# Bonus sums of the first two chunks by TensorE, state decay on ScalarE, one weight split less ahead of the first tile

## The chip, the cores and the metric

One core of a Trainium2 chip runs the whole kernel. The metric is the device time of one execution in microseconds. Engines are named as the profile names them: PE is TensorE, DVE VectorE, ACT ScalarE, POOL GpSimd, SP SyncE, which here only issues transfers.

## The reference, cut to what matters

```
for t in range(S):                       # attention with decay, B 2, H 8, S 768, D 48
    cur = u[None] * kt outer vt          # the bonus: only for the step itself
    y[t] = rt . (state + cur)
    state = w * state + kt outer vt
x = y as [1536 tokens, 384]
x = sum over 4 experts e: p[:, e] * (relu(x @ w1[e]) @ w2[e])     # hidden 1024
out = elu(x @ w_in) @ w_out              # hidden 2048, alpha 1
```

All in 32-bit floats. The share of the bonus in y at token t and head h is a0[t, h] * v[t], with a0[t, h] the sum over the head's 48 elements of r * u * k.

## The kernel before, in words

The attention runs in 12 chunks of 128 tokens, six for each batch. In each chunk r is scaled by the powers of w (table `T`) and k by their inverses (table `Kd`) in the layout with tokens along the columns (`rkT`, lines 204 to 207). `s2` multiplies them to scores, and `s2p` copies the scores under a mask (`copy_predicated`) into the tile `A`, whose diagonal holds a0. `s1u` makes `uk` = r * u * k in the layout with tokens along the partitions (`rk`, 384 columns of r and 384 of k), `s1d` reduces it to a0, and the diagonals are written as the identity times a0: the even heads on GpSimd (line 242), the odd ones on ScalarE (`s1e`, line 248) in chunks 2 and 3, all on GpSimd after that. For chunks 0 and 1, `A` is zeroed at the start, and the bonus comes in at the end instead: `va` = v * a0 on VectorE, added by TensorE in `s3i`. `s3s` brings the state to the next chunk: `Z` = sum of the chunk + old state, `S` = `Z` times w to the 128th, both on VectorE.

Ahead of the loop all of chunks 0 and 1 is done, and part of chunk 2. Then `layers` runs six hidden layers (four experts, two halves of the last one) over token tiles; the first tile has 256 tokens and eight steps f = 0 to 7. At step f: `st1` (line 684), `evac` (`hh` on ScalarE, `hl` on VectorE), then a piece of the attention from the list `steps` (f = 0: scores of chunk 2, preparation of chunk 3; f = 1: `s3(2)`; f = 2: scores of chunk 3; f = 3: `s3(3)`; f = 4: preparation of chunk 4; f = 6: scores of chunk 4; f = 7: `s4(3)`, which writes `xh` and `xl` of tokens 256 to 511 from the tile `xs`), then `st2` of step f - 2 (line 722), and last `work(0.9)`, which makes one split.

A split takes one weight slice `raw` (128 x 768), writes its high part `wh` on ScalarE and its low part `wl` on VectorE (or on the engine `weng`), and then issues the load of the slice three further on, since there are three `raw` buffers. The slices are numbered here from 0 in the order in which they are made: (0,1,0), (0,1,1), (0,2,0), (0,1,2), (0,2,1), (0,1,3), (0,2,2), (0,2,3). The middle number is 1 for `st1` and 2 for `st2`, and the last is f // 2. Eight slots hold eight split slices, and the first tile uses all eight.

Each engine takes its instructions in the order written. SP's queue holds the loads in program order; `s3` of an odd chunk stores `yT` to `xd`, and the load of `xs` behind it waits for that store to land.

## Time and profile before

| what | value |
|---|---|
| median of 3 runs | 653.62 us (653.33 to 654.23) |
| the profiled execution | 653.03 us, of which the span 651.1 us |
| TensorE matmuls | 639.2 us, 98% of the span |
| VectorE, ScalarE, GpSimd | 334.1, 216.7, 214.6 us |

The profile gives, for one execution, start and duration of each instruction, the idle time ahead of it with the instruction that ended it, and for a transfer the time from issue to landing. Times in timelines count from the start of the span. PEld is the loading of weights into TensorE.

### The profile page before, as it was taken

To read this page: it belongs to the slowest core of one execution; us is meant where nothing else is said; L and a number is where in the kernel's file an instruction comes from. 1 tells how busy PE (TensorE), PEld (TensorE's weight loads), DVE (VectorE), ACT (ScalarE), POOL (GpSimd) and SP (SyncE) were. 2 spreads that over 40 slices of the span, in tenths; PEclk is the share of its full clock that TensorE was granted. 3 is DMA by queue.
4 is the path that set the end of the run, shared out by engine and by line. 5 is a ranking of instruction groups with operands and counts; after the bars stand their busy time and mean duration, and the time that the engine had idled before them with its cause. 6 is when DMAs were issued, how large, how long until landed. Compare 5 with 4: busy or idle time off the path is not lost.

```text
span 651.1 us, 9435 instructions
## 1 busy us (share of the span) xinstructions
PE 639.2 (98%) x3825; PEld 537.1 (82%) x3825; DVE 334.1 (51%) x472; ACT 216.7 (33%) x370; POOL 214.6 (33%) x178
## 2 busy tenths in 40 slices
PE   9799999999999999999999999999999999999996
PEld 6699998988888888888888888888888888888885
DVE  7975665346454545554545456566667553222221
ACT  5532222333211132211122112123645564544441
POOL 7954773100031212130311122242754434333331
PEclk9999999999999999999999999999999999999998
DMA  8883562343230233421216231318441342001011
GB/s 257 248 288 120 160 175 76 144 122 122 72 97 1 98 120 118 159 88 48 98 49 229 92 138 52 97 35 312 188 146 44 102 145 98 0 1 49 1 49 53
DMA packets 27735, 73.10 MB, mean 112 GB/s; under 512 B 3154, under 2 KB 8580, under 8 KB 27684
## 3 DMA queue, kind: packets, MB, share of 16 engines
q1 hardware_dynamic: 22928, 59.80, 28.6%
q10 hardware_dynamic: 4756, 12.61, 5.1%
q8 instruction: 32, 0.52, 0.3%
q14 instruction: 19, 0.16, 0.1%
HBM read 55.47 MB, written 16.93 MB: 111 GB/s over the span
## 4 chain that ended last, share of the span: by engine, by line
PE 95%; DVE 3%; issue 1%; ACT 0%; DVEq 0%
PE ph L684 45%; PE po L722 45%; PE pa L263 1%; PE ph L102 1%; PE pa L334 1%; PE pa L325 1%; DVE rkT L206 1%; PE po L334 1%; PE ph L285 1%; DVE A L270 0%; DVE wl L533 0%; DVE a L232 0%; DVE acc L772 0%; DVE hl L697 0%; DVE xl L496 0%
## 5 line engine op out<-in xcount | busy, mean ns | idle before, releaser
L722 PE MATMUL po<-hh,wh 128*128 128x512 f32 (+1 forms) x480 | 177.4, 370 | 0.0
L722 PE MATMUL po<-hl,wh 128*128 128x512 f32 (+1 forms) x480 | 176.5, 368 | 0.0
L722 PE MATMUL po<-hh,wl 128*128 128x512 f32 (+1 forms) x480 | 176.5, 368 | 0.0
L684 PE MATMUL ph<-xh,wh 128*128 128x512 f32 (+1 forms) x480 | 174.5, 369 | 1.5 <-DVE xl L496 0.8
L684 PE MATMUL ph<-xh,wl 128*128 128x512 f32 (+1 forms) x480 | 173.8, 368 | 0.0
L696 ACT ACTIVATE hh<-ph 128x512 fp32r<-128x512 f32 (+1 forms) x112 | 60.2, 537 | 269.3 <-PE ph L684 266.4
L697 DVE SCALAR_TENSOR_TENSOR hl<-ph,hh 128x512 fp32r<-128x512 f32 (+1 forms) x112 | 68.5, 613 | 154.6 <-ACT hh L696 154.2
L684 PE MATMUL ph<-xl,wh 128*128 128x512 f32 (+1 forms) x480 | 124.6, 368 | 0.0
L684 PEld LDWEIGHTS ph<-xh,wh 128*128 128x128 f32 x480 | 90.4, 188 | 17.6 <-DVE hl L697 1.0
L722 PEld LDWEIGHTS po<-hh,wh 128*128 128x128 f32 x480 | 90.4, 188 | 16.5 <-issue 1.5
L722 PEld LDWEIGHTS po<-hl,wh 128*128 128x128 f32 x480 | 90.4, 188 | 15.0
L722 PEld LDWEIGHTS po<-hh,wl 128*128 128x128 f32 x480 | 90.4, 188 | 15.0
L684 PEld LDWEIGHTS ph<-xh,wl 128*128 128x128 f32 x480 | 90.5, 188 | 14.9
L709 POOL TENSOR_TENSOR hl<-g,hh 128x512 fp32r<-128x512 f32 x48 | 63.2, 1318 | 117.4 <-ACT hh L708 109.3
L684 PEld LDWEIGHTS ph<-xl,wh 128*128 128x128 f32 x480 | 85.9, 188 | 15.2 <-DVE xl L496 0.2
L595 POOL TENSOR_TENSOR nl<-a,wide 128x768 fp32r<-128x768 f32 x16 | 29.9, 1870 | 173.5 <-issue 105.8
L706 DVE SCALAR_TENSOR_TENSOR g<-m,ph 128x512 f32<-128x512 f32 x48 | 33.0, 686 | 104.4 <-ACT m L704 100.1
L744 POOL TENSOR_TENSOR acc<-acc,t 128x512 f32<-128x512 f32 x27 | 34.2, 1297 | 72.8 <-DVE t L743 72.8
L708 ACT CAST hh<-g 128x512 fp32r<-128x512 f32 x48 | 29.9, 622 | 43.0 <-DVE g L706 43.0
L703 ACT ACTIVATE m<-ph 128x512 f32<-128x512 f32 x48 | 28.7, 598 | 43.4 <-PE ph L684 36.4
L533 DVE TENSOR_TENSOR wl<-raw,wh 128x768 fp32r<-128x768 f32 x31 | 30.7, 1004 | 7.2 <-ACT wh L532 6.7
L704 ACT ACTIVATE m<-m 128x512 f32<-128x512 f32 x48 | 30.4, 632 | 1.5
(116 smaller groups left out, 478.9 us busy)
## 6 DMA issues: line engine op xcount, KB each, us to landing
raw<-in_ws_dram SPq DMA_DIRECT2D x32, 384.0 KB, 4.3
wide<-in_ws_dram SPq DMA_DIRECT2D x16, 768.0 KB, 5.1
w<-nh ACTq DMA_DIRECT2D x16, 384.0 KB, 2.5
w<-nl ACTq DMA_DIRECT2D x16, 384.0 KB, 5.6
wh<-w SPq DMA_DIRECT2D x16, 384.0 KB, 6.0
wl<-w SPq DMA_DIRECT2D x16, 384.0 KB, 6.8
rk<-in_rkv_dram SPq DMA_DIRECT2D x12, 384.0 KB, 6.4
rkT<-in_rkT_dram SPq DMA_DIRECT2D x10, 448.0 KB, 6.0
```

The costliest lines, as they stand in the source:

```text
L533: self.weng.tensor_tensor(out=lo, in0=t, in1=hi.bitcast(F32), op=ALU.subtract)
L595: nc.gpsimd.tensor_tensor(out=lo, in0=af, in1=cf, op=ALU.add)
L684: nc.tensor.matmul(ph[:, 0:n], a[:, kk, c0:c0 + P], b[:, kk], start=q == 0, stop=q == 3 * KD - 1)
L696: nc.scalar.activation(hh[:, 0:n], ph[:, 0:n], AF.Relu)
L697: nc.vector.scalar_tensor_tensor(out=hl[:, 0:n], in0=ph[:, 0:n], scalar=0.0, in1=hh[:, 0:n].bitcast(F32), op0=ALU.max, op1=ALU.subtract)
L703: nc.scalar.activation(m, ph, AF.Relu, scale=-1.0)
L704: nc.scalar.activation(m, m, AF.Exp, scale=-1.0)
L706: nc.vector.scalar_tensor_tensor(out=gg, in0=m, scalar=-1.0, in1=ph, op0=ALU.add, op1=ALU.max)
L708: nc.scalar.copy(hh, gg)
L709: nc.gpsimd.tensor_tensor(out=hl, in0=gg, in1=hh.bitcast(F32), op=ALU.subtract)
L722: nc.tensor.matmul(po, a[:, ff, i * P:(i + 1) * P], b[:, 0:n], start=f == 0 and q == 0 and not i * n % TB, stop=f == NF - 1 and q == 2 and ...
L744: nc.gpsimd.tensor_tensor(out=a, in0=a, in1=t[:, 0:n], op=ALU.add)
```

## The change

The bonus sums a0 of chunks 0 and 1 are made from the scaled `rkT`: VectorE multiplies r by k (`s1p`), and TensorE sums each head's 48 rows with a table `U2` = u * w as the moving operand (`s1a`); the factor w makes up for the powers that the scaling left. The result is written to the diagonals of `A` (even heads GpSimd, odd heads ScalarE), as in chunks 2 and 3. So r by token isn't loaded for these chunks (`load_kv`), `va` and `s3i` go, and `A` isn't zeroed. `vp` has two buffers. The table `Kt` comes from a reversed copy of `T` (`Tr`), not from `Kd`. The decay is multiplied in ahead, by ScalarE (`s3w`, four activations), so that VectorE has one addition for each chunk. Four warm matmuls are left out. The second split ahead of the loop, on GpSimd, is left out. The first `ph` buffer of the loop is the other one.

```diff
--- before.py
+++ after.py
@@ -74,11 +74,15 @@
         self.ub = c.tile([P, DM], F32, name="ub")
         self.ur = c.tile([1, DM], F32, name="ur")
         self.one = c.tile([1, P], F32, name="one")
-        self.vp = c.tile([P, 112 + 160 * H], F32, tag="xs", name="vp")
+        self.vp = [
+            c.tile([P, 112 + 160 * H], F32, tag="xs", name="vp0"),
+            g.xp.tile([P, 112 + 160 * H], F32, tag="acc2", name="vp1")]
         self.Sp = c.tile([P, 96 + 192 * NP], F32, tag="yT", name="Sp")
         self.mask = c.tile([P, P], U8, name="mask")
-        self.rkT, self.rk, self.v, self.va, self.pa, self.st, self.px = ({} for _ in range(7))
-        self.S = self.Sv = self.zero = None
+        self.ud = c.tile([P, NP], F32, name="ud")
+        self.U2 = c.tile([P, NP, 2], F32, name="U2")
+        self.rkT, self.rk, self.v, self.a0, self.pa, self.st, self.px = ({} for _ in range(7))
+        self.S = self.wS = self.zero = None
 
         self.own = [(self.ps, f"pa{i}") for i in range(3)] + [(g.pop, "po2")]
         self.banks = self.own[:3] + [(g.pop, f"po{i}") for i in range(KD)] + [(g.php, "ph0")]
@@ -116,6 +120,11 @@
         self.rk[ci] = t = self.p3.tile([P, 2, DM], F32, tag="rk", name="rk")
         self.g.nc.sync.dma_start(out=t, in_=self.g.rkv[ci, :, 0:2])
 
+    def load_kv(self, ci):
+        t = self.p3.tile([P, 2, DM], F32, tag="rk", name="rk")
+        self.g.nc.sync.dma_start(out=t, in_=self.g.rkv[ci, :, 1:3])
+        self.rk[ci], self.v[ci] = t, t[:, 1]
+
     def load_v(self, ci):
         self.v[ci] = t = self.p4.tile([P, DM], F32, tag="v", name="v")
         self.g.nc.sync.dma_start(out=t, in_=self.g.rkv[ci, :, 2])
@@ -123,15 +132,14 @@
     def setup_loads(self):
         g, nc = self.g, self.g.nc
         nc.scalar.dma_start(out=self.ur, in_=g.u.rearrange("h d -> (h d)").rearrange("(o n) -> o n", o=1))
+        nc.scalar.dma_start(out=self.ud, in_=g.ud)
         nc.sync.dma_start(out=self.wd, in_=g.wd)
         for ci in range(2):
             self.load_T(ci)
             self.load_T2(ci, 0)
             self.load_T2(ci, 1)
-        self.load_rk(0)
-        self.load_v(0)
-        self.load_rk(1)
-        self.load_v(1)
+        self.load_kv(0)
+        self.load_kv(1)
 
     def setup_tables(self):
         g, nc = self.g, self.g.nc
@@ -160,6 +168,12 @@
                 out=Kd[:, :, n:2 * n], in0=Kd[:, :, 0:n],
                 in1=Kd[:, :, n - 1:n].to_broadcast([P, NP, n]), op=ALU.mult)
 
+    def setup_u2(self):
+        for j in range(2):
+            a = slice(64 * j, 64 * j + D)
+            self.g.nc.gpsimd.tensor_tensor(
+                out=self.U2[a, :, j], in0=self.ud[a], in1=self.T[a, :, 1], op=ALU.mult)
+
     def setup_masks(self):
         nc = self.g.nc
 
@@ -172,17 +186,16 @@
 
     def setup_zeros(self):
         nc = self.g.nc
-        for t in self.A:
-            for j in range(2):
-                nc.scalar.copy(t[:, j].rearrange("s p t -> s (p t)"), self.zero)
-        for i in range(0, self.vp.shape[1], 512):
-            t = self.vp[:, i:min(i + 512, self.vp.shape[1])]
-            nc.scalar.copy(t, self.zero[:, 0:t.shape[1]])
+        for vp in self.vp:
+            for i in range(0, vp.shape[1], 512):
+                t = vp[:, i:min(i + 512, vp.shape[1])]
+                nc.scalar.copy(t, self.zero[:, 0:t.shape[1]])
 
     def setup_rest(self):
         nc = self.g.nc
         for t in self.kp:
             nc.gpsimd.memset(t.rearrange("t p j d -> t (p j) d")[:, :, D:64], 0.0)
+        nc.gpsimd.memset(self.U2, 0.0)
         nc.gpsimd.memset(self.Sp, 0.0)
         for t in self.Sb:
             nc.gpsimd.memset(t[:, :, D:64], 0.0)
@@ -195,8 +208,10 @@
     def setup_kt(self):
         g, nc = self.g, self.g.nc
         pk = self.bank()
+        Tr = self.c.tile([P, NP, P], F32, name="Tr")
+        nc.scalar.copy(Tr, self.T[:, :, P - 1::-1])
         for p in range(NP):
-            nc.tensor.transpose(pk[:, p * P:(p + 1) * P], self.Kd[:, p, :], g.ident)
+            nc.tensor.transpose(pk[:, p * P:(p + 1) * P], Tr[:, p, :], g.ident)
         nc.scalar.copy(self.Kt.rearrange("t p j d -> t (p j d)"), pk)
 
 
@@ -207,7 +222,7 @@
         self.st.setdefault(ci, {})["rk"[i]] = self.rkT[ci][:, i]
 
     def heads(self, ci, i):
-        return self.rk[ci][:, i].rearrange("t (h d) -> t h d", h=H)
+        return self.rk[ci][:, i if ci > 1 else 0].rearrange("t (h d) -> t h d", h=H)
 
 
     def s1k(self, ci):
@@ -227,26 +242,35 @@
 
 
     def s1d(self, ci):
-        nc = self.g.nc
-        a0 = self.p2.tile([P, H], F32, tag="a0", name="a0")
-        nc.vector.tensor_reduce(out=a0, in_=self.st[ci]["uk"], axis=AX.X, op=ALU.add)
-        if ci < 2:
-
-            self.va[ci] = va = self.p2.tile([P, DM], F32, tag="va", name="va")
-            nc.vector.tensor_tensor(
-                out=va.rearrange("t (h d) -> t h d", h=H), in0=self.v[ci].rearrange("t (h d) -> t h d", h=H),
-                in1=a0.rearrange("s (h o) -> s h o", o=1).to_broadcast([P, H, D]), op=ALU.mult)
-            return
-        self.a0 = a0
+        self.a0[ci] = a0 = self.p2.tile([P, H], F32, tag="a0", name="a0")
+        self.g.nc.vector.tensor_reduce(out=a0, in_=self.st[ci]["uk"], axis=AX.X, op=ALU.add)
         for j in range(1 if ci < 4 else 2):
-            nc.gpsimd.tensor_tensor(
-                out=self.A[ci % 2][:, j], in0=self.g.ident.rearrange("s (a t) -> s a t", a=1).to_broadcast([P, NP, P]),
-                in1=a0.rearrange("s (p j o) -> s p j o", j=2, o=1)[:, :, j].to_broadcast([P, NP, P]), op=ALU.mult)
+            self.s1g(ci, j)
+
+    def s1g(self, ci, j):
+        self.g.nc.gpsimd.tensor_tensor(
+            out=self.A[ci % 2][:, j], in0=self.g.ident.rearrange("s (a t) -> s a t", a=1).to_broadcast([P, NP, P]),
+            in1=self.a0[ci].rearrange("s (p j o) -> s p j o", j=2, o=1)[:, :, j].to_broadcast([P, NP, P]), op=ALU.mult)
 
     def s1e(self, ci):
         for p in range(NP):
             self.g.nc.scalar.activation(
-                self.A[ci % 2][:, 1, p, :], self.g.ident, AF.Copy, scale=self.a0[:, 2 * p + 1:2 * p + 2])
+                self.A[ci % 2][:, 1, p, :], self.g.ident, AF.Copy, scale=self.a0[ci][:, 2 * p + 1:2 * p + 2])
+
+
+    def s1p(self, ci):
+        self.pr = self.p2.tile([P, NP, P], F32, tag="pr", name="pr")[0:112]
+        st = self.st[ci]
+        self.g.nc.vector.tensor_tensor(out=self.pr, in0=st["r"][0:112], in1=st["k"][0:112], op=ALU.mult)
+
+    def s1a(self, ci):
+        nc = self.g.nc
+        pq = self.g.php.tile([P, 512], F32, tag="ph1", name="ph1")[:, 0:H]
+        for p in range(NP):
+            nc.tensor.matmul(
+                pq[:, 2 * p:2 * p + 2], self.pr[:, p, :], self.U2[0:112, p, :], start=True, stop=True)
+        self.a0[ci] = a0 = self.p2.tile([P, H], F32, tag="a0", name="a0")
+        nc.scalar.copy(a0, pq)
 
     def s1(self, ci):
         self.s1h(ci, 0)
@@ -291,24 +315,26 @@
         nc = self.g.nc
         if pu is None:
             return
-        old, v = self.Sv, nc.vector
-        w = self.T[0:112, :, P:P + 1]
         src = pu[0:112, 0:NP * D].rearrange("q (p e) -> q p e", p=NP)
         if not ci:
-            self.Sv = self.Sp[0:112, 96:].rearrange("q (p n) -> q p n", p=NP)[:, :, 0:96].rearrange(
+            Sv = self.Sp[0:112, 96:].rearrange("q (p n) -> q p n", p=NP)[:, :, 0:96].rearrange(
                 "q p (j e) -> q p j e", j=2)
             for j in range(2):
                 a = slice(64 * j, 64 * j + D)
-                v.tensor_tensor(out=self.Sv[a, :, j, :], in0=src[a], in1=w[a].to_broadcast([D, NP, D]), op=ALU.mult)
+                nc.scalar.copy(Sv[a, :, j, :], src[a])
             return
         self.S = self.Sb[ci % 2]
-        self.Sv = self.S[0:112, :, 0:D]
+        out = self.S[0:112, :, 0:D]
         if ci % NCB:
-            z = self.p2.tile([P, NP, D], F32, tag="Z", name="Z")[0:112]
-            for a, o in [(slice(0, 64), old[:, :, 0]), (slice(64, 112), old[:, :, 1])] if ci == 1 else [(slice(0, 112), old)]:
-                v.tensor_tensor(out=z[a], in0=src[a], in1=o[a], op=ALU.add)
-            src = z
-        v.tensor_tensor(out=self.Sv, in0=src, in1=w.to_broadcast([112, NP, D]), op=ALU.mult)
+            nc.vector.tensor_tensor(out=out, in0=src, in1=self.wS, op=ALU.add)
+        else:
+            nc.vector.tensor_copy(out, src)
+
+    def s3w(self, src):
+        self.wS = self.p2.tile([P, NP, D], F32, tag="wS", name="wS")[0:112]
+        for p in range(NP):
+            self.g.nc.scalar.activation(
+                self.wS[:, p, :], src[:, p, :], AF.Copy, scale=self.T[0:112, p, P:P + 1])
 
     def s3(self, ci, more=False):
         g, nc = self.g, self.g.nc
@@ -339,6 +365,8 @@
             self.yT = self.c.tile([P, 2, 2, 2 * P], F32, tag="yT", name="yT")
         for j in range(2):
             nc.scalar.copy(self.yT[0:112, :, j, o:o + P], py[j][0:112])
+        if c < NCB - 2:
+            self.s3w(self.S[0:112, :, 0:D])
         if o:
 
             t0 = (ci - 1) * P
@@ -352,33 +380,29 @@
 
     def s3v(self, ci):
         self.g.nc.scalar.copy(
-            self.vp[:, 112:].rearrange("t (h n) -> t h n", h=H)[:, :, 0:D],
+            self.vp[ci][:, 112:].rearrange("t (h n) -> t h n", h=H)[:, :, 0:D],
             self.v[ci].rearrange("t (h d) -> t h d", h=H))
 
     def s3f(self, ci):
         g, nc = self.g, self.g.nc
         st = self.st[ci]
         self.px[ci] = px = self.bank().rearrange("q (k t) -> q k t", k=4)
-        for kk in range(KD):
-
-            at = lambda n, t: [(i, 64 * t - n * i) for i in range(DM // n) if 64 * t - n < n * i < 64 * (t + 1)]
-            ops = [[], []]
+        at = lambda n, t: [(i, 64 * t - n * i) for i in range(DM // n) if 64 * t - n < n * i < 64 * (t + 1)]
+        ops = [[], [], [], []]
+        for t in range(2 * KD):
+            if ci:
+                ops[t % 2] += [
+                    (t // 2, self.Sp[0:112, 96 + 192 * p + a:][:, 0:64], st["r"][0:112, p, :]) for p, a in at(96, t)]
+            ops[2 + t % 2] += [
+                (t // 2, self.vp[ci][:, 112 + 160 * h + a:][:, 0:64], self.A[ci % 2][:, h % 2, h // 2, :])
+                for h, a in at(D, t)]
+        ops = [ops[i] + ops[2 + i] for i in range(2)]
+        m = len(ops[0])
+        assert m == len(ops[1])
+        for n in range(m):
             for i, o in enumerate(ops):
-                t = 2 * kk + i
-                if ci:
-                    o += [(self.Sp[0:112, 96 + 192 * p + a:][:, 0:64], st["r"][0:112, p, :]) for p, a in at(96, t)]
-                o += [(self.vp[:, 112 + 160 * h + a:][:, 0:64], self.A[ci % 2][:, h % 2, h // 2, :])
-                      for h, a in at(D, t)]
-            for n in range(max(map(len, ops))):
-                for i, o in enumerate(ops):
-                    if n < len(o):
-                        nc.tensor.matmul(
-                            px[64 * i:64 * (i + 1), kk, :], *o[n], start=not n and not kk, stop=False)
-
-    def s3i(self, ci):
-        for kk in range(KD):
-            self.g.nc.tensor.matmul(
-                self.px[ci][:, kk, :], self.va[ci][:, kk * P:(kk + 1) * P], self.g.ident, start=False, stop=kk == KD - 1)
+                kk, a, b = o[n]
+                nc.tensor.matmul(px[64 * i:64 * (i + 1), kk, :], a, b, start=not n, stop=n == m - 1)
 
     def s3x(self, ci):
         self.g.put_x(0, ci * P, P, self.px[ci][:, 0:KD, :], self.g.nc.vector)
@@ -861,20 +885,21 @@
             self.hp, self.hw = ctx.enter_context(tc.tile_pool(name="hp", bufs=3)), 256
             actx = ExitStack()
             at = Fast(self, actx)
-            at.warm(WARM - 4)
+            at.warm(WARM - 8)
             at.setup_zeros()
             at.setup_loads()
             dp = self.probs_in()
+            at.setup_rest()
             make_identity(nc, self.ident)
             self.load_next()
+            at.load_T(2)
             at.load_rk(2)
             self.load_next()
-            at.load_T(2)
             at.load_v(2)
             at.setup_masks()
             at.setup_tables()
-            at.setup_rest()
             at.setup_tables2()
+            at.setup_u2()
 
             def load(c):
                 if c < NCH:
@@ -884,47 +909,48 @@
 
             at.s1h(0, 0)
             at.s1h(0, 1)
-            at.setup_ub()
             at.setup_kt()
             at.s2(0)
-            at.s3v(0)
+            at.s1p(0)
+            at.s1a(0)
+            at.setup_ub()
             at.s1h(1, 0)
             at.s1h(1, 1)
-            at.s2p(0)
             at.s1k(0)
-            at.s1u(0)
-            at.s1u(1)
+            at.s1g(0, 0)
+            at.s1e(0)
+            at.s3v(0)
+            at.s1p(1)
             load(3)
             at.load_rk(3)
             self.load_next()
+            pu = at.s3u(0)
             at.s2(1)
-            at.s2p(1)
-            pu = at.s3u(0)
+            at.s1a(1)
             at.s3s(0, pu)
+            at.s1g(1, 0)
+            at.s1e(1)
+            at.s2p(0)
             at.s3f(0)
             at.s3v(1)
-            at.s1d(0)
             at.s1k(1)
+            at.s2p(1)
+            self.work(0.1)
+            at.s3w(pu[0:112, 0:NP * D].rearrange("q (p e) -> q p e", p=NP))
             at.s1u(2)
             at.s1k(2)
-            at.s1d(1)
-            self.work(0.1)
+            at.s3x(0)
             at.s3f(1)
-            at.s3i(0)
-            at.s3x(0)
-            at.s3i(1)
             at.nbank = 2
             pu = at.s3u(1)
+            at.s1h(2, 0)
             at.s3x(1)
-            at.s1h(2, 0)
             at.s1h(2, 1)
             self.probs(dp)
             at.s1d(2)
             at.s3s(1, pu)
-            self.weng = nc.gpsimd
-            self.work(0.1)
-            self.weng = nc.vector
-            at.banks, at.nbank = at.own, 0
+            at.s3w(at.S[0:112, :, 0:D])
+            at.banks, at.nbank, self.nph = at.own, 0, 1
             load(4)
             at.load_rk(4)
 
```

## Rows read from the trace of the kernel before

**Rows 1.** The page's first line.

```profile
span 651.1 us, 9435 instructions
```

**Rows 2.** Windows: stretch, length, busy us of each engine, clock, transfer share, GB/s.

```profile
17.88:31.00 13.12, 10.04 (x154) 8.64 (x155) 13.01 (x22) 6.92 (x17) 12.19 (x13) 1.00 0.78 252
31.00:651.00 620.00, 613.64 (x3482) 518.03 (x3480) 306.62 (x423) 200.38 (x337) 189.14 (x142) 1.00 0.32 105
```

**Rows 3.** Waits of PE, 17.5 to 32 us: us in total, times, longest.

```profile
PE pa L263 <- issue: 1.1, 1, 1.1
...
PE pa L263 <- PE ph L684: 0.8, 1, 0.8
PE ph L657 <- DVE hl L697: 0.6, 1, 0.6
PE ph L684 <- DVE hl L697: 0.6, 1, 0.6
```

**Rows 4.** Groups by line, 0 to 45 us: busy us, mean ns | idle before.

```profile
L248 ACT ACTIVATE A<-ident,a 128x128 f32<-128x128 f32 x8 | 2.6, 390 | 1.8 <-DVE a L232 1.8
...
L236 DVE TENSOR_TENSOR va<-v,a 128x384 f32<-128x384 f32 x2 | 2.1, 1028 | 0.1
```

**Rows 5.** Timeline of DVE, 19 to 28 us: start, us, instruction.

```profile
19.48 0.71 DVE L206 TENSOR_TENSOR rkT<-rkT,Kd 112x512 f32<-112x512 f32 x1
...
20.57 0.71 DVE L309 TENSOR_TENSOR Z<-pa,Sp 64x192 f32<-64x192 f32 x2
21.32 0.74 DVE L311 TENSOR_TENSOR S<-Z,T 112x192 f32<-112x192 f32 x1
...
22.43 1.35 DVE L270 COPY_PREDICATED A<-mask,pa 128x512 f32<-128x512 uint8 x2
...
23.81 1.45 DVE L206 TENSOR_TENSOR rkT<-rkT,T 112x512 f32<-112x512 f32 x1
25.19 1.50 DVE L206 TENSOR_TENSOR rkT<-rkT,Kd 112x512 f32<-112x512 f32 x1
...
27.07 0.94 DVE L533 TENSOR_TENSOR wl<-raw,wh 128x768 fp32r<-128x768 f32 x1
```

**Rows 6.** Timeline of ACT, 43 to 45 us.

```profile
43.86 0.38 ACT L696 ACTIVATE hh<-ph 128x256 fp32r<-128x256 f32 x1 [2.99 <-PE ph L684]
44.14 0.83 ACT L495 CAST xh<-xs 128x768 fp32r<-128x768 f32 x1
```

**Rows 7.** Timeline of POOL, 21 to 24 us.

```profile
21.80 1.95 POOL L533 TENSOR_TENSOR wl<-raw,wh 128x768 fp32r<-128x768 f32 x1
```

**Rows 8.** Timeline of PE: first matmul of steps 2 and 3, and of tile two.

```profile
24.64 0.38 PE L684 MATMUL ph<-xh,wh 128*128 128x256 f32 x1
...
30.39 0.39 PE L684 MATMUL ph<-xh,wh 128*128 128x256 f32 x1 [0.56 <-DVE hl L697]
...
45.02 0.38 PE L684 MATMUL ph<-xh,wh 128*128 128x256 f32 x1
```

**Rows 9.** Timeline of SP's queue, 32 to 42 us: start and length of the issues.

```profile
32.69 0.33 SPq L507 DMA_DIRECT2D raw<-in_ws_dram  x1
34.23 0.83 SPq L346 DMA_DIRECT2D xd<-yT  x2
39.08 0.39 SPq L350 DMA_DIRECT2D xs<-xd  x1
...
41.04 0.94 SPq L507 DMA_DIRECT2D raw<-in_ws_dram  x2
```

**Rows 10.** Line 117, the issue at 40.56 us (`rk`): its landing.

```profile
DMA to landing us min/median/max: 6.6/6.6/6.6
```

**Rows 11.** Line 507, the issue at 41.5 us (`raw`): its landing.

```profile
DMA to landing us min/median/max: 7.7/7.7/7.7
```

**Rows 12.** Line 507, the issue at 28.0 us (`raw`): its landing.

```profile
DMA to landing us min/median/max: 4.3/4.3/4.3
```

**Rows 13.** Line 630, the issue at 4.2 us (`dp`): its landing.

```profile
DMA to landing us min/median/max: 6.5/6.5/6.5
```

## The prediction

> **What bounds the kernel now.** I read the span first [rows 1], then busy times and granted clock by stretch, to find where TensorE is not the limit. From 31 us on TensorE works 613.64 of 620 us, at a granted clock of 1.00; what is missing is nearly all the tail after its last matmul. Nothing that VectorE, ScalarE or GpSimd save there can show. Between 17.88 and 31 us it is another picture: VectorE is busy 13.01 of 13.12 us and TensorE 10.04 [rows 2]. So the change can pay only if the first 31 us get shorter, or cost if a new wait appears in the full part. TensorE's waits of that stretch name the four gaps: 1.1 us before the scores of chunk 2, 0.8 before those of chunk 3, and twice 0.6 for `hl` [rows 3]. Together 3.1 us: that is all there is to win after the first expert matmul.
>
> **The change part by part.**
>
> *Start, to the first expert matmul.* Removed: GpSimd's `uk` products of chunks 0 and 1, VectorE's two reductions and its two `va` products (2.1 us alone), TensorE's twelve `s3i` matmuls and four of the warm ones. Added in series, for each of the two chunks: a product on VectorE, four small matmuls, a copy of `a0`, then the diagonals, half on GpSimd and half on ScalarE, and only then `copy_predicated`. Before, these copies could start as soon as the scores were there, because `A` was zero. ScalarE's half is four activations, 2.6 us for eight in the trace [rows 4], so 1.3 us for each chunk; the zeroing of `A` that it no longer does lay under the loads anyway. VectorE loses 2.1 us and more, ScalarE's chain gains 2.6 plus the state copies and `ub`, which now stands in ScalarE's queue ahead of the diagonals. I take the two as equal, with bounds of -2.1 and +2.6. So chunk 2's `rkT` products end on VectorE where they did, at 20.19 (19.48 + 0.71) [rows 5].
>
> *State decay.* VectorE had `Z` and then `S`: 20.57 to 22.06. Now one addition is left, half of the 0.71 of the two `Z`, so `S` of chunk 1 is ready at 20.93: 1.1 us sooner. But ScalarE must then run `s3w`, four activations of 48 columns. No row shows that shape: above nothing, and below the 1.3 us of four with 128 columns; I take 1.0, near the upper row, since most of a short activation is not columns. What queues behind: `hh` of the first expert tile (0.38, as [rows 6] shows for a later one) and then the odd diagonals of chunk 2 (1.3), which in the trace were made meanwhile. So `s3w` ends at 22.0, `hh` at 22.35, the diagonals at 23.65, and the second half of `copy_predicated` at 24.35, where before it ended at 23.78 [rows 5]. Later `s3w` calls lie in ScalarE's idle time.
>
> *The second weight split leaves the start.* I hold this for the costliest line of the diff. GpSimd made the low part of split 1 (`(0,1,1)`, needed by `st1` of f = 2) in 1.95 us from 21.80 [rows 7]. Now the start makes only split 0, and each later one comes one step f later. Split 1 falls into VectorE's slot at the end of f = 0, where the trace has split 2: 27.07 to 28.01. That slot lies 4.23 us behind the end of `copy_predicated`; in it the two `rkT` products of chunk 3 took 1.45 and 1.50 while GpSimd worked on `wl` and `uk`, against 0.71 for the one at 19.48 [rows 5]. GpSimd now has `uk` behind it by then, so I take 1.5 us off: the slot ends at 24.35 + 2.7 = 27.05. `st1` of f = 2 began at 24.64 and now waits for it. From there to `st1` of f = 3 the trace has 5.75 us (24.64 to 30.39 [rows 8]) with 2.0 us of waits in it, so 3.75 of work: f = 3 begins at 30.8, 0.4 later than before. The three later gaps are closed, and one new one has eaten them.
>
> *The load behind the split.* A split also issues the load that takes its buffer, three slices on. Split 4 issues the load of slice 7, the last that the first tile needs. In the trace split 4 is part of f = 2, and the load goes out at 32.69, ahead of the `xd` store (34.23) and the `xs` load that waits for that store to land (39.08). Now split 4 is part of f = 3 and its load stands in SP's queue behind `xd`, `xs`, and the `rkT`, `v` and `rk` of chunk 6: in the place of the load that went out at 41.04 [rows 9]. The landing of that one is not shown. Its neighbours are: the `rk` issued at 40.56 took 6.6 us (47.2) [rows 10], the `raw` issued second, at 41.5, took 7.7 (49.2) [rows 11]; so 48.2, and 1.0 us for each of these 384 KB loads. Against this, `xd` no longer has slice 7 ahead of it: I take 1.0 off, and add the 0.4 from above: slice 7 lands at 47.6.
>
> What waits for it: ScalarE takes its queue in order. At f = 6 it now has `wh` of slice 7, and behind that `hh` of f = 7 and `xh` of tokens 256 to 511. In the trace ScalarE stood idle 2.99 us until `hh` at 43.86, then `xh` at 44.14 for 0.83 [rows 6], and TensorE began the second tile at 45.02 [rows 8]. Now: 47.6, plus 0.83 for `wh` (same size as that `xh`), plus 0.28 to `xh`, plus 0.88 to the first matmul: 49.6. VectorE's `wl`, `hl` and `xl` queue in the same way. TensorE's queue has nothing else to do in between: the second matmuls of f = 6 need slice 7 themselves. What TensorE loses before 45 us on the way is swallowed by this wait.
>
> *The sum.* 49.6 - 45.0 = +4.6 us. Everything after 45 us is full TensorE work in the same order, so it moves by 4.6. The profiled execution took 653.03 (span 651.1 and 1.9 around it): 657.6. The median shown is 653.62, 0.6 higher, so **658.2**. A difference under 0.2% (1.3 us) is about what a measurement of this kernel can't tell from none.
>
> *A rule that speaks against this.* The two landings above are in the order of issue (47.2, 49.2) [rows 10, 11], and 658.2 rests on that order. The Trainium skill ("DMA: Bandwidth & Descriptors", section "Queues, rings and completion order") says that completion is not first in, first out for one issuing engine: a later transfer may finish before an earlier one. By that rule slice 7 need not wait for the loads ahead of it; no row here shows an overtaking, so it is the first rival, with its time from rows.
>
> **The rivals.**
>
> *The load overtakes (slower by little).* Slice 7 takes what a load took with less around it, 4.3 us [rows 12], from its issue at 40.4 (41.04 + 0.4 - 1.0): 44.7, and the second tile starts at 46.7: +1.7, so 655.3; if the startup also gains a little, within 0.2%. For it: its 384 KB alone are short. Against it: 6.6 and 7.7 us of the neighbours.
>
> *Faster: the start shrinks.* VectorE bounds the stretch to 31 us, and the change takes 2.1 (`va`), 1.1 (`Z`, `S`) and 1.5 (less disturbance) from it, GpSimd's `wl` too. If ScalarE's chain isn't the longer one, the start is 2.1 us shorter and the gaps close. TensorE then reaches f = 3 some 3 us sooner, the store, `xs` and slice 7 come 3 us sooner as well, and if slice 7 also overtakes, the second tile starts 1.7 us before its old time (1.7 - 0.4 - 3.0), 651.9; with no wait on slice 7 at all the whole 3 us stay: 650.6. It decides if slice 7 lands before about 43 us. Against it: the chain above for ScalarE and slot 27.05.
>
> *Slower by more: `ud`.* `U2` needs the new load `ud`, on ScalarE's queue while SP's loads fill the engines. The one such load in the trace, `dp`, took 6.5 us [rows 13]. GpSimd waits for it with `kp` of chunk 0 behind. If `ud` takes as long, the start loses some 2 us, and with it the store: 660.2.
>
> **How the numbers follow.** Forecast 0.57, overtaking 0.14, faster 0.19, `ud` 0.10. The likeliest alone: 655.9 to 660.5, from -2.1 and +2.6 of the start, each weakened by the waits that follow. For 8 in 10 the range reaches down into the faster case: 652.6 to 661.0. Faster by over 0.2%: 0.19; within: 0.10 (from overtaking with a gain at the start, and weak forms of the faster case); slower: 0.71.
>
> **What would show it.** Right: `wh` of the eighth slice begins after 46 us, with ScalarE's wait put down to the `raw` load; SP issues that load after `xs`; TensorE idles 3 us or more before the second tile; `st1` of f = 2 waits for VectorE's `wl`; the gaps of 0.8 and 0.6 are gone; from there to the end the length is as before. Wrong, and with it the forecast: the eighth `raw` issued ahead of `xs`, or landing by 43 us; the first expert matmul more than 2 us off 17.9; a granted clock under 1.00 in the first 18 us, with four warm matmuls fewer; or `s3w` at far under 1 us.

## The result, and the profile after

The changed kernel takes 660.76 us (median of 7 runs, 657.9 to 663.08) against 653.62 for the kernel before (7 runs): a ratio of 1.0101, 95% interval 1.008 to 1.0122. It is 7.1 us slower. The profiled execution took 659.59 us. Read in the order of the prediction: the span first, then TensorE's clock and busy time by stretch, then TensorE's waits.

The first line of the changed kernel's page:

```profile
span 657.7 us, 9468 instructions
```

Windows of the changed kernel (stretch, length, busy us of each engine, clock, transfer share, GB/s):

```profile
0.00:10.50 10.50, 8.88 (x68) 4.62 (x70) 6.53 (x18) 6.26 (x12) 7.44 (x22) 0.99 0.77 227
10.50:20.30 9.80, 9.80 (x105) 9.37 (x103) 4.82 (x7) 5.77 (x19) 5.69 (x6) 0.50 0.99 271
...
30.70:33.90 3.20, 3.20 (x40) 2.77 (x39) 1.87 (x3) 3.20 (x11) 3.12 (x3) 0.50 0.90 301
...
60.00:651.00 591.00, 591.00 (x3197) 497.87 (x3197) 286.61 (x389) 196.86 (x339) 175.69 (x131) 1.00 0.30 99
```

The second of these stretches in the kernel before:

```profile
10.50:20.30 9.80, 7.48 (x104) 6.64 (x102) 9.66 (x14) 3.32 (x6) 9.44 (x10) 1.00 1.04 272
```

From 60 us to the end of the matmuls TensorE is never idle, and in the kernel before it was idle there for 0.5 us in all: what is lost is lost ahead of it. VectorE, which was busy 9.66 of 9.80 us from 10.5 to 20.3, is now down to 4.82. What the change saves on VectorE is real. But TensorE is busy all of that time at a granted clock of 0.50, which is 1.2 of 2.4 GHz, where the kernel before had 1.00; and it is at 0.50 again from 30.7 to 33.9. A busy engine is not a fast one.

TensorE's waits between 17.5 and 60 us (in total, times, longest):

```profile
PE ph L708 <- ACT xh L519: 2.2, 2, 2.1
PE ph L708 <- DVE wl L557: 1.7, 1, 1.7
PE po L746 <- DVE wl L557: 0.5, 1, 0.5
```

None of the four gaps of [rows 3] is left; three new waits stand in their place. The first is the second tile's, the other two are for low parts of splits.

The changed kernel's timeline of TensorE (start, length, instruction, idle before it):

```profile
6.85 1.10 PE L287 MATMUL pa<-rkT 48*64 48x128 f32 x32
...
10.98 1.99 PE L287 MATMUL po<-rkT 48*64 48x128 f32 x32
...
17.30 1.92 PE L405 MATMUL pa<-rkT,Sp 112*64 112x128 f32 x16
...
21.80 0.39 PE L708 MATMUL ph<-xh,wh 128*128 128x256 f32 x1 [0.16 <-ACT xh L519]
...
29.63 0.39 PE L708 MATMUL ph<-xh,wl 128*128 128x256 f32 x1 [1.69 <-DVE wl L557]
...
34.56 0.28 PE L708 MATMUL ph<-xh,wh 128*128 128x256 f32 x1
...
51.82 0.39 PE L708 MATMUL ph<-xh,wh 128*128 128x256 f32 x1 [2.08 <-ACT xh L519]
```

The first expert matmul (`st1` of f = 0) in the kernel before:

```profile
17.91 0.35 PE L684 MATMUL ph<-xh,wh 128*128 128x256 f32 x1 [0.84 <-DVE xl L496]
```

Scores of chunk 0 take 1.10 us at 6.85, the same 32 matmuls for chunk 1 take 1.99 at 10.98: that is the clock. The first expert matmul is at 21.80 where before it was at 17.91: 3.9 later. Step f = 3 is at 34.56, 4.2 later, and the second tile at 51.82, 6.8 later [rows 8].

The changed kernel's SP queue (start and length of each issue), and the landing of the load issued at 43.5 us:

```profile
35.89 0.33 SPq L531 DMA_DIRECT2D raw<-in_ws_dram  x1
...
38.30 0.83 SPq L374 DMA_DIRECT2D xd<-yT  x2
41.56 0.39 SPq L378 DMA_DIRECT2D xs<-xd  x1
...
43.04 0.38 SPq L121 DMA_DIRECT2D rk<-in_rkv_dram  x1
43.51 0.86 SPq L531 DMA_DIRECT2D raw<-in_ws_dram  x2
```

```profile
DMA to landing us min/median/max: 6.4/6.4/6.4
```

And its timeline of ScalarE, with the state decay (line 336), `hh` (720), the odd diagonals (257), and `wh` of slice 7 (556):

```profile
23.69 1.01 ACT L336 ACTIVATE wS<-S,T 112x48 f32<-112x48 f32 x4 [1.95 <-DVE S L329]
24.61 0.36 ACT L720 ACTIVATE hh<-ph 128x256 fp32r<-128x256 f32 x1
24.88 1.27 ACT L257 ACTIVATE A<-ident,a 128x128 f32<-128x128 f32 x4
...
30.26 1.01 ACT L336 ACTIVATE wS<-S,T 112x48 f32<-112x48 f32 x4 [2.20 <-DVE S L329]
...
49.93 0.83 ACT L556 CAST wh<-raw 128x768 fp32r<-128x768 f32 x1 [4.18 <-DMA raw<-in_ws_dram]
50.67 0.38 ACT L720 ACTIVATE hh<-ph 128x256 fp32r<-128x256 f32 x1
50.95 0.82 ACT L519 CAST xh<-xs 128x768 fp32r<-128x768 f32 x1
```

This is the chain that the prediction describes. The load of slice 7 now stands behind `xd`, `xs` and the three loads of chunk 6 [rows 9], it lands at 49.9, and `wh`, `hh` and `xh` follow in ScalarE's order; the second tile starts 0.87 us after `xh` began. Before, `xh` was at 44.14 [rows 6].

### The profile page after: what moved, and what is told of

Its sections match the earlier page's. It is cut to its first block, busy times and chain, and to the rows that moved or that the text cites. A ratio compares the mean times of both kernels' runs of the same rounds, so it can differ in the third digit from the quotient of the medians.

```text
span 657.7 us, 9468 instructions
## 1 busy us (share of the span) xinstructions
PE 645.3 (98%) x3825; PEld 543.3 (83%) x3825; DVE 324.5 (49%) x460; ACT 226.1 (34%) x414; POOL 209.5 (32%) x178
## 4 chain that ended last, share of the span: by engine, by line
PE 94%; DMA 2%; DVE 2%; ACT 1%; issue 0%; SPq 0%; POOL 0%; POOLq 0%; DVEq 0%
PE po L746 44%; PE ph L708 44%; PE pa L287 1%; DMA raw<-in_ws_dram 1%; DMA rk<-in_rkv_dram 1%; PE pa L360 1%; PE pa L351 1%; PE po L360 1%; PE ph L309 1%; PE pa L405 1%; PE ph L405 0%; DVE rkT L221 0%; DVE acc L796 0%; ACT wS L336 0%; PE po L287 0%
## 5 line engine op out<-in xcount | busy, mean ns | idle before, releaser
L557 DVE TENSOR_TENSOR wl<-raw,wh 128x768 fp32r<-128x768 f32 x32 | 30.7, 974 | 13.3 <-ACT wh L556 12.8
L251 POOL TENSOR_TENSOR A<-ident,a 128x512 f32<-128x512 f32 x20 | 22.4, 1137 | 37.1 <-DVE a L246 33.1
```

What stands on the lines that cost most here:

```text
L251: self.g.nc.gpsimd.tensor_tensor(out=self.A[ci % 2][:, j], in0=self.g.ident.rearrange("s (a t) -> s a t", a=1).to_broadcast([P, NP, P]), i ...
L557: self.weng.tensor_tensor(out=lo, in0=t, in1=hi.bitcast(F32), op=ALU.subtract)
```

## The experiments

Three theories were held apart. **L** (the load): leaving out the second split moves slice 7's load behind `xs` in SP's queue, and that sets the time. **C** (the clock): the late start with its fallen clock sets it. **Q** (ScalarE's queue), formed after the first runs: each later state decay stands in ScalarE's queue ahead of `wh` and `hh` and waits there for VectorE's `S`. Each ratio is against the kernel before on the same chip, with its 95% interval.

**Second split back.** The changed kernel with this ahead of the loop:

```diff
+            self.weng = nc.gpsimd
+            self.work(0.1)
+            self.weng = nc.vector
             at.banks, at.nbank, self.nph = at.own, 0, 1
```

> The changed kernel with the second weight split back in the start, on GpSimd, as in the kernel before. Theory L (the missing split is what costs: step f = 2 waits 1.7 us for its low part, and slice 7's load goes out behind the xs load, so that TensorE waits 2.1 us for the second tile): slice 7's load goes out ahead of xs, both waits are gone, about 656.5 us. Theory C (the half clock from 10 to 20 us is what costs, and the split is hidden): 659 to 661 us, first expert matmul still 3 to 4 us later than before.

Measured: 658.71 us (657.78 to 660.91), 1.0074 [1.0059, 1.0089], 2 us under the changed kernel. SP's queue and TensorE's longest wait in this kernel:

```profile
38.30 0.33 SPq L531 DMA_DIRECT2D raw<-in_ws_dram  x1
41.43 0.83 SPq L374 DMA_DIRECT2D xd<-yT  x2
```

```profile
PE ph L708 <- DVE hl L721: 2.6, 1, 2.6
```

Slice 7's load went out at 38.30, ahead of `xd`, and no wait for it is left. But another came: st1 of f = 3 waits 2.6 us for `hl`. Neither expectation came as it stood: the time is 2.2 over the 656.5 of L and 0.3 under the range of C, and the first expert matmul, at 21.77, is as late as C said. So L holds for the place of the load, and something else hides behind it. ScalarE's timeline of this kernel shows what:

```profile
32.26 1.01 ACT L336 ACTIVATE wS<-S,T 112x48 f32<-112x48 f32 x4 [3.50 <-DVE S L329]
33.18 0.82 ACT L556 CAST wh<-raw 128x768 fp32r<-128x768 f32 x1
33.90 0.37 ACT L720 ACTIVATE hh<-ph 128x256 fp32r<-128x256 f32 x1
```

The decay of chunk 2 waits 3.50 us for `S`, and `hh`, without which VectorE can't make `hl`, stands behind it.

**The split alone.** The kernel before without its second split, and nothing else of the change:

```diff
-            self.weng = nc.gpsimd
-            self.work(0.1)
-            self.weng = nc.vector
```

> The kernel before with one edit, its second split left out of the start. Theory L: first expert matmul at 17.9 us as before, but step f = 2 waits for VectorE until 27 us or later, slice 7's load goes out behind xs at about 41 us and lands at about 48, second tile at 49 to 50 instead of 45.0: +4 to +5 us, about 658. Theory C: nothing light was added, the clock stays at 1.00, and the time is within 1 us of 653.6.

Measured: 658.65 us (658.12 to 659.61), 1.007 [1.0057, 1.0083]: 4.7 us more than before, for one line. SP's queue and ScalarE's timeline of this kernel:

```profile
38.02 0.39 SPq L350 DMA_DIRECT2D xs<-xd  x1
...
39.98 0.86 SPq L507 DMA_DIRECT2D raw<-in_ws_dram  x2
```

```profile
46.96 0.83 ACT L532 CAST wh<-raw 128x768 fp32r<-128x768 f32 x1 [5.81 <-DMA raw<-in_ws_dram]
```

TensorE's timeline at the second tile, and the window from 50 to 55 us:

```profile
48.84 0.58 PE L684 MATMUL ph<-xh,wh 128*128 128x256 f32 x1 [3.66 <-ACT xh L495]
```

```profile
50.00:55.00 5.00, 5.00 (x28) 5.00 (x27) 2.02 (x4) 0.66 (x2) 3.13 (x4) 0.58 0.22 76
```

Its start is not to blame: the granted clock is 1.00 up to 45 us. TensorE's wait for `xh` is 3.7 us, and the one for `wl` of split 1 is 1.6. The second tile is 3.8 us later than before (48.84 against 45.02); the rest of the 4.7 comes behind that wait, where the clock is 0.58 from 50 to 55 us. L is shown: the wait by the trace, the price by the time.

**Slice 7's load ahead of `xs`.** The changed kernel with the `xs` load of chunk 3 held back until split 4 has issued its own:

```diff
+            def load_xs(xs=self.xs):
+                nc.sync.dma_start(out=xs, in_=...)
+            if ci == 3:
+                self.late_xs = load_xs
...
+                if u == 0 and t0 == 0 and f == 4:
+                    at.late_xs()
```

> The changed kernel with the first xs load issued after split 4's work instead of in the attention step, so that slice 7's load no longer waits behind the landing of the store. Theory L: slice 7's load goes out at about 41 us instead of 43.5, lands by 47.5, and TensorE's wait of 2.1 us for the second tile is gone or becomes a short one for xs itself: about 658.7 to 659.5. If slice 7's place in the queue doesn't matter (only the split's place does): 660.8.

Measured: 657.22 us (656.05 to 657.87), 1.0047 [1.0034, 1.0059]: 3.5 us under the changed kernel, by one load's place. SP's queue of this kernel:

```profile
41.11 0.38 SPq L536 DMA_DIRECT2D raw<-in_ws_dram  x1
41.66 0.38 SPq L379 DMA_DIRECT2D xs<-xd  x1
```

`wh` of slice 7 starts at 47.30 instead of 49.93, the second tile at 49.82 instead of 51.82, and of TensorE's waits for `xh` none is over 0.2 us. The gain in the medians is larger than L's expectation (1.3 to 2.1 us). The two traces show 2.0 us of it, at the second tile; where the other 1.5 come from is not shown.

**The decay alone.** The kernel before with the state decay on ScalarE as in the change. Its table for k is left as it was, so that its state lacks the factor w to the 128th; the instructions that are timed are all there.

```diff
-            src = z
-        v.tensor_tensor(out=self.Sv, in0=src, in1=w.to_broadcast([112, NP, D]), op=ALU.mult)
+            nc.vector.tensor_tensor(out=out, in0=src, in1=self.wS, op=ALU.add)
...
+        if c < NCB - 2:
+            self.s3w(self.S[0:112, :, 0:D])
```

> The kernel before with the state decay alone moved to ScalarE (one addition on VectorE, four activations on ScalarE, as in the changed kernel). By the prediction's step: S of chunk 1 about 1.1 us sooner, then hh and the odd diagonals of chunk 2 behind the activations, so copy_predicated ends 0.6 us later; the two rkT products of chunk 3 and the low part follow. Between -0.5 and +0.8 us: 653.4 to 654.7. If VectorE's saved work is what counts: -1 us or more, 653 or less.

Measured: 656.97 us (656.53 to 657.32), 1.0047 [1.0034, 1.006]. That is 3.2 us slower and a miss: this part had been given next to no price. VectorE's and ScalarE's timelines of this kernel:

```profile
28.76 0.41 DVE L701 SCALAR_TENSOR_TENSOR hl<-ph,hh 128x256 fp32r<-128x256 f32 x1
29.09 0.34 DVE L305 TENSOR_TENSOR S<-po,wS 112x192 f32<-112x192 f32 x1
```

```profile
29.53 1.01 ACT L312 ACTIVATE wS<-S,T 112x48 f32<-112x48 f32 x4 [3.51 <-DVE S L305]
...
31.17 0.37 ACT L700 ACTIVATE hh<-ph 128x256 fp32r<-128x256 f32 x1
```

`S` is the last of VectorE's items of that step, behind `wl` and `hl`. ScalarE was idle for 3.51 us with `hh` of f = 2 queued behind; st1 of f = 3 then waits 2.3 us for `hl` and starts at 32.93 (30.39 in [rows 8]), and from 32 to 39 us the clock is 0.53 in the mean. That is Q, without any other part of the change.

**The decay moved.** The changed kernel with the second split back, and each later decay issued at the beginning of the next chunk's s3, where `S` is about to be read anyway:

```diff
     def s3(self, ci, more=False):
...
+        if 0 < c < NCB - 1:
+            self.s3w(self.S[0:112, :, 0:D])
...
-        if c < NCB - 2:
-            self.s3w(self.S[0:112, :, 0:D])
```

> The changed kernel with its second split on GpSimd again, and each later state decay moved on ScalarE from the end of its chunk's s3 to the next chunk's s3, right before the chunk's state matmuls read the state; the computation is the same. Theory Q (ScalarE's queue: the decay of S stands ahead of wh and hh and waits for VectorE's S): the wait of st1 for hl of 2.6 us that the version with the second split on GpSimd has goes away and so does the fall of the clock behind it; the time is 655.0 to 657.0, 2 to 3.5 us under that version's 658.7. Rival (hl is late because VectorE itself is behind its work, not because hh is): the wait for hl stays, 658 to 659.5.

Measured: 655.5 us (654.38 to 656.17), 1.0024 [1.0001, 1.0047]: 3.2 us less for the order of one engine's queue. TensorE's waits in this kernel from 17.5 to 60 us:

```profile
PE ph L681 <- DVE hl L721: 1.6, 1, 1.6
PE ph L708 <- DVE hl L721: 0.7, 2, 0.5
```

The 2.6 us are gone, and the clock is 1.00 in each five-microsecond stretch from 20 to 60 us. A 1.6 us wait has moved to the small transpose of `pn` (line 681); it was 0.6 there. Q is shown.

The trace of this kernel also shows C by itself. Its start has the changed kernel's instructions, and its scores of chunk 1 begin at the same time (10.97 and 10.98). But in this execution the clock, 0.50 from 11 to 16 us, is back at 1.00 from 18 us on, and in the changed kernel's it is 0.50 up to 20:

```profile
17.29 1.30 PE L405 MATMUL pa<-rkT,Sp 112*64 112x128 f32 x16
```

The same 16 matmuls took 1.92 there, from 17.30, and the first expert matmul comes at 20.51 instead of 21.80. So 1.3 us of the start are the clock's alone, and they are not a gain of the moved decay.

**The decay moved, on the kernel before.** The kernel before with the decay on ScalarE in the moved place, and the table for k from the reversed `T`:

```diff
+        Tr = self.c.tile([P, NP, P], F32, name="Tr")
+        nc.scalar.copy(Tr, self.T[:, :, P - 1::-1])
...
+        if 0 < c < NCB - 1:
+            self.s3w(self.S[0:112, :, 0:D])
```

> The kernel before with the state decay on ScalarE (three scaled copies fewer on VectorE per chunk, the table for k taken from the reversed T), each later decay moved to the next chunk's s3. The computation is the reference's. Theory Q (the 3.2 us that the same edit cost with the decay at the end of each s3 came from hh and wh standing behind it): 652.5 to 654.0, no wait of st1 for hl over 0.5 us near 33 us. Rival (the decay costs by itself, by 1.0 us of ScalarE per chunk or by what VectorE does instead): 655.5 to 657.

Measured: 655.5 us (652.75 to 657.37), 1.0026 [1.0008, 1.0044], on the edge of the rival's range. TensorE's wait of 2.3 us for `hl` is down to 0.3, so what Q says of it holds. Three of its nine executions (652.75 to 653.84) lie in the range of Q, six above it. In the profiled one (655.03) the rest sits in the start: TensorE waits 1.2 us for `Tr`, its clock is 0.66 in the mean from 10 to 15 us, the first expert matmul comes at 20.32 (17.91 before) and the second tile at 47.43, both 2.4 late. The run joined two edits; with the decay on ScalarE but the old table the first expert matmul was at 17.76, so that it is the reversed table that goes with the late start. This start has 14 warm matmuls and no bonus sums by TensorE, and its clock fell all the same. With this table the edit doesn't pay.

**Three tries to hold the clock in the start.** Each is the changed kernel with one edit: `WARM - 4` in place of `WARM - 8` (as many warm matmuls as before); `U2` 128 columns wide, of which two are read; nine more warm matmuls between the steps of the start.

```diff
-            at.warm(WARM - 8)
+            at.warm(WARM - 4)
```

> The changed kernel with 14 warm matmuls instead of 10. If the four missing warm matmuls are why the granted clock falls at 10 us, it stays at 1.00 to 20 us and the time is about 656.5. If the light matmuls of the bonus sums and the waits are why (theory C in its other form), it falls as before: 660 or a little more, since four matmuls are added. Theory L: no change, 660.

```diff
-        self.U2 = c.tile([P, NP, 2], F32, name="U2")
+        self.U2 = c.tile([P, NP, P], F32, name="U2")
```

> The changed kernel with 128 instead of 2 moving columns in each of the bonus sums' matmuls (the added columns of U2 are zero and their results are not used). In a row of 128-column products the weight loads set the pace anyway, so the sums should last no longer at full clock. Theory C: the clock stays at 1.00 from 10 to 20 us, first expert matmul at 18 to 19 us instead of 21.8, about 656.5 us. Theory L: no change but the longer fill of U2, 660 to 661.

```diff
             at.s1p(0)
+            at.warm(1)
             at.s1a(0)
+            at.warm(2)
             at.setup_ub()
+            at.warm(2)
...
             at.s1a(1)
+            at.warm(4)
```

> The changed kernel with nine more warm matmuls (512 columns each, results unused) in the places of the start where TensorE has little to do: one after the Kt transposes, two ahead of the first bonus sums, two after ub, four after the second bonus sums. Theory C (the half clock of the start costs most of its 3.9 us): the clock stays at 1.00 from 10 to 20 us and the first expert matmul comes at 18.5 to 19.5 us instead of 21.8; since TensorE then waits longer for slice 7, only about 1 to 2 us of it reach the end: 658.5 to 660. If the clock falls all the same, or the ScalarE chain is the longer one: 660 to 661, first expert matmul at 21 or later.

Measured: 660.58 (1.0105 [1.009, 1.0121]), 660.84 (1.009 [1.0071, 1.0108]) and 660.78 us (1.0108 [1.0084, 1.0132]): no change in any of them. The clock fell in the profiled execution of all three, to a mean of 0.51, 0.50 and 0.52 from 11 to 16 us. These runs don't decide about C, for the thing to be changed did not change there. Whether it fell in every execution is not shown: for the filled start the profiled one is the slowest of six (664.3, mean clock over the whole execution 0.985), and three others took 659.13 to 659.74 at 0.995; for the wide `U2` it is the slowest too (662.28, 0.992), and two others took 658.09 and 658.1 at 0.996 and 0.994. The first one still tells something: its first expert matmul was at 19.84, 2.0 sooner, and the second tile only 0.6 sooner, at 51.19, with a wait of 3.4 us.

**The filled start with the second split back.** The last of these edits on the version with the second split on GpSimd.

> The same nine matmuls and the second split back in the start. Theories L and C together: with slice 7 no longer late, the shorter start reaches the end in full, 2.5 to 3.5 us below the 658.7 of the second split alone: 655 to 656. If the ScalarE chain, not the clock, makes the start late: 658 to 659.

Measured: 661.24 us (661.15 to 661.96), 1.0116 [1.0102, 1.0131]. The clock fell all the same (0.60 from 11 to 16 us), TensorE still waits 2.3 us for `hl`, and the first expert matmul is at 22.28, 0.5 later than without the fill. A miss.

**All three, and more warm matmuls.** The wide `U2` and the nine matmuls between the steps, with 15 warm matmuls at the head in place of 10 (the two expectations that follow say "15 more"; it is 15 in all, 5 more):

```diff
-            at.warm(WARM - 8)
+            at.warm(WARM - 3)
```

> The changed kernel with 15 more warm-up matmuls at its head, nine more between the steps of the start, and U2 held 128 columns wide so that the diagonal's matmuls have 128 columns (two of each are read); what is computed is the same. Each of the three alone left the granted clock at 0.50 from about 11 to 16 us or longer. Theory C (the clock falls because TensorE stands idle between the steps of the start): with all three the clock stays at 1.00 to 20 us, s2 takes 1.1 us instead of 2.0, the first expert matmul comes at about 19 to 20 us instead of 21.80, and the time is 658 to 660, 1 to 2 us under the changed kernel's. Rival (the start is late whatever the clock does, because the second tile sets the time by slice 7's load, or because the clock falls all the same): 660 to 662.

Measured: 660.06 us (659.28 to 661.77), 1.0108 [1.0091, 1.0124]. Windows and TensorE's timeline of this kernel:

```profile
10.50:20.30 9.80, 9.33 (x150) 7.85 (x149) 6.14 (x9) 6.74 (x21) 6.68 (x7) 1.00 0.97 298
```

```profile
19.11 0.39 PE L708 MATMUL ph<-xh,wh 128*128 128x256 f32 x1 [0.16 <-ACT xh L519]
...
50.31 0.39 PE L708 MATMUL ph<-xh,wh 128*128 128x256 f32 x1 [2.93 <-ACT xh L519]
```

Now the clock holds, and the start is 2.7 us sooner, both as C expected. The time, 660.06, lies where the two ranges meet, and the ratio is no better than the changed kernel's: the second tile still waits for slice 7 (1.5 us sooner, with 0.8 us more of waiting), and the clock falls behind that wait, to a mean of 0.67 from 50 to 55 us; 33% of 5 us is 1.65 by estimate, more than the 1.5 gained. So C's fall is real, and as long as slice 7's load stands where it stands, mending it gives next to nothing.

**The dense start where nothing waits for slice 7.** The same start on the version with the second split back and the decay moved:

> The changed kernel with the second split on GpSimd again, each later state decay moved to the next chunk's s3, and the dense start of the version with 15 more warm-up matmuls, nine more between the steps and U2 of 128 columns; the computation is the same. In the version without the dense start nothing waits for slice 7's load and the first expert matmul is at 20.51; with the dense start alone it was at 19.11 (17.91 before), and what it gained was lost at slice 7's load. Theory (with both queue effects gone an earlier start is worth its full length): first expert matmul near 19.1, time 653.5 to 654.6, about 1.4 us under the 655.5 of the version without the dense start and within 0.2% of before. Rival (an earlier start only meets the next late thing, on VectorE or in SP's queue): 655 to 656.

Measured: 653.62 us (652.66 to 655.67, 12 runs) against 654.18, 0.9995 [0.9983, 1.0006]: level with the kernel before, and 1.9 us under the version without the dense start. Windows and TensorE's timeline of this kernel:

```profile
10.50:20.30 9.80, 9.39 (x149) 7.53 (x148) 5.64 (x9) 7.62 (x22) 6.67 (x6) 1.00 1.02 286
```

```profile
19.61 0.38 PE L708 MATMUL ph<-xh,wh 128*128 128x256 f32 x1 [0.16 <-ACT xh L519]
```

The first expert matmul is 1.7 us later than before, the second tile (45.78) only 0.8: the closed gaps give 0.9 back. No version beat the kernel before.

| kernel | first expert matmul, us | second tile, us | median, us | ratio |
|---|---|---|---|---|
| before | 17.91 | 45.02 | 653.62 | 1 |
| changed | 21.80 | 51.82 | 660.76 | 1.0101 |
| + second split | 21.77 | 52.21 | 658.71 | 1.0074 |
| + decay moved | 20.51 | 46.43 | 655.5 | 1.0024 |
| + dense start | 19.61 | 45.78 | 653.62 | 0.9995 |

The three steps take off 2.1, 3.2 and 1.9 us, together the 7.1 that the change cost. (The matmuls' times are those of one profiled execution. That of the third row took 659.98 us, 1.3 over its median, and that of the second 659.59, 1.2 under; so their second tiles don't show the 2.1. That of the fourth took 654.38, 1.1 under, with the earlier return of the clock told above; so it makes the step to it look too large, and the next too small.)

## Why the prediction was right, and where it was not

The direction was right, and 660.76 lies inside 652.6 to 661.0; the size was taken 2.6 us too small (658.2). The time is 0.24 us under the upper end. Of the prediction's own signs, the late `wh`, the place of the load, the wait for `wl` and the closed gaps came; the idle time before the second tile is 2.1 us and not 3 or more; and two of the signs that were to make it wrong came as well, the first expert matmul 3.9 us off 17.9 and a clock under 1.00 in the first 18 us. So the largest term was right, and that the time lies in the range owes something to luck. The range itself has a slip: its lower likely bound, 655.9, is 2.3 under 658.2, though the start was to take off 2.1 at most, and that weakened. By its steps:

*The load behind the split: right, and shown.* The edit alone costs 4.7 us, where the sum had 4.6. The nearness of the two is in part luck: the sum put all of it at the second tile, which came 3.8 later, and the rest is the clock behind the wait, which the sum does not have. In the changed kernel `xs` follows `xd` by 3.26 us instead of 4.85, so that 1.6 came off there, and 1.0 was assumed. From the landing (49.9) to the second tile 1.9 us passed, and 2.0 were assumed.

*Split 1 in VectorE's slot: right in kind, and in time by two errors that cancel.* VectorE's timeline of the changed kernel:

```profile
25.35 1.58 DVE L294 COPY_PREDICATED A<-mask,pa 128x512 f32<-128x512 uint8 x2
...
26.95 0.63 DVE L221 TENSOR_TENSOR rkT<-rkT,T 112x512 f32<-112x512 f32 x1
27.49 0.75 DVE L221 TENSOR_TENSOR rkT<-rkT,Kd 112x512 f32<-112x512 f32 x1
...
28.63 0.94 DVE L557 TENSOR_TENSOR wl<-raw,wh 128x768 fp32r<-128x768 f32 x1
```

The two products of chunk 3 take 0.63 and 0.75 where they took 1.45 and 1.50 [rows 5]: 1.57 off, and 1.5 was assumed (with the split back on GpSimd they take 1.17 and 1.50). Taken back by the 3.9 us of the start, `copy_predicated` ends at 23.0 (24.35 assumed) and the slot at 25.7 (27.05 assumed): VectorE had time to spare in the longer start (it waits 1.39 us for `xh` ahead of 21.78), and `S` of chunk 1, with which that chain begins, was ready at 19.8 by this count, not at 20.93. But from there to f = 3 it is 4.93 us (29.63 to 34.56) instead of 3.75, with a clock of 0.50 from 30.7 to 33.9, which loses, by estimate, 1.6 of 3.2. So f = 3 comes at 30.7 in the prediction's time, where it had 30.8.

*The overtaking load: did not come.* Slice 7's load, issued after `xs`, `rkT`, `v` and `rk`, landed at 49.9, behind them all: at 45.2, 46.9, 47.2 and 48.9 by their issues and landings of 3.6, 4.9, 4.7 and 5.9 us. What hung on the rule of the Trainium skill ("DMA: Bandwidth & Descriptors", section "Queues, rings and completion order"), that a later transfer may finish before an earlier one, was the time 655.3; the rule allows an overtaking, and these five loads show none.

*The start: this is the term that was mis-sized.* "I take the two as equal, with bounds of -2.1 and +2.6"; it was +3.9, outside the bounds. The chain of the bonus sums is not the larger part of it. With the clock held, and the extra matmuls that this took, the start is 1.2 to 1.7 us longer than before, well inside the bounds. The other 2.2 to 2.7 go with the granted clock, which is 0.50 from 10.5 to 20.3 us; for 1.3 of them two executions of the same start show the clock alone as the cause. The prediction named that case as one that would make it wrong, gave it no time and no chance, and so slice 7's load went out at 43.51 instead of 40.4. Of the 3.9 us, 3.1 arrive there, and 2.2 at the second tile (51.82, not 49.6), since the landing took 6.4 and not 7.2. `ud`, the third rival, landed after 4.0 us and held up GpSimd for 0.85, not 2: too little to be the cause.

*The state decay: half right.* `s3w` takes 1.01 us, as assumed; `S`, `hh` and the diagonals of chunk 2 come in the order and at the distances that were worked out. "Later `s3w` calls lie in ScalarE's idle time" is the step that failed. The idle time is there, but an instruction that waits in it holds all that is queued behind. ScalarE's idle time before `hh` was time in which `hh` could start at once; with the decay ahead of it, it could not. In the changed kernel no wait for `hl` shows it, and st1 of f = 2 is itself 1.7 us late for `wl`; what it costs there was not measured. With the split back, it costs 3.2. By the rule that an added wait is costed by what is queued behind it, each call should have been followed, not the first alone.

*Faster because VectorE is relieved: fell.* VectorE is relieved, and the gaps of 0.8 and 0.6 are closed, which was foreseen. They come back as 0.9 us in the last version, where nothing new stands in their place; 1.7 us of longer start stand against it.

So of two errors, one in the start and one in ScalarE's queue, the changed kernel shows the first alone, and that reduced; the second came out only when the second split was put back. For the same reason a mended start gives next to nothing by itself: its 2.7 us become 2.3 at slice 7's load (41.19), 1.5 at the second tile, and are then taken by the clock behind the longer wait.

What stays open is which property of the start lets the clock fall. The kernel before had 14 warm matmuls, and the clock held; the changed one has 10. As many as before, wide `U2`, or filling, each alone, did not hold it in the execution that was profiled; all of them together with still more warm matmuls did. Which pair would have done was not tried, nor was the moved decay without the second split.

## What to carry to other kernels

A piece of work that issues a load belongs to the load's queue as much as to its engine: before you move it, write down what the queue holds between the old and the new place, and above all any load in it that waits for a store. A wait at the head of an in-order queue costs what stands behind it, so move an operation to where its input is needed and not to where the engine looks idle. Where several late things lie under one wait, mending one of them shows nothing: mend the last wait first, and then measure the others again.

## What the runs showed of the hardware

In the changed kernel the granted clock of TensorE fell to 0.50 (1.2 of 2.4 GHz) between 10.0 and 10.5 us, after a stretch in which TensorE had been busy 8.88 of 10.5 us. In two executions of the same start it was back at 1.00 by 18 us in one and after 20 us in the other. In the first 10 us it was busy 8.44; in the changed kernel with the dense start it was busy 8.49, and there the clock held at 1.00. The busy time of the profile does not tell the two apart. It was also lower behind longer waits: behind the 3.7 us before the second tile in the kernel before without its second split it was 0.74 in the mean from 45 to 50 us and 0.58 from 50 to 55, so that TensorE at 0.58 lost, by estimate, 2.1 us (42% of 5) on top of the wait. Behind the 2.08 us wait at the same place of the changed kernel it stayed at 1.00, yet behind the 1.69 us wait for `wl` at 29.63, with other gaps ahead of it (TensorE busy 3.31 of the five us from 25), it fell to 0.50. So a wait in front of full TensorE work can cost more than its own length, and how much is read from the clock behind it.
